# Decode attention with a gated FFN on one core: engine programs as loops over quarter heads, and the FFN moved ahead of the last head's values

## The chip, the cores and the metric

The kernel runs on one core of one Trainium2 chip. The metric is the device time of one execution in microseconds (us). The profile is one execution recorded by the hardware, and its span is about 1.8 us shorter than the device time.

Short names: PE is the matrix engine, DVE the vector engine, ACT the scalar engine, SP the engine that issues the loads. Sixteen DMA engines carry out each load together: in the packet records of the traces each load ends with 16 completions, one from each.

## The reference, cut to what matters

One token attends over a long cache: 16 query heads share 8 key and value heads of 65,536 positions and 256 channels, in bf16. A gated FFN of width 1792 runs on the same normalised token.

```python
# ...
Hq, Hkv, Sk, Dh = 16, 8, 65536, 256
q = (x @ wq)                                      # 16 heads, 2 for each key head
scores = einsum("bhqd,bhkd->bhqk", q, k) * Dh ** -0.5
o = einsum("bhqk,bhkd->bhqd", softmax(scores), v)
a = o.reshape(1, 1, Hq * Dh) @ wo                 # 4096 x 448
# ...
g = silu(x_sel @ w_gate); u = x_sel @ w_up        # 448 x 1792 each
y = (g * u) @ w_down * sigmoid(r)                 # 1792 x 448
return x + a + (xn + y)
```

The caches are 2 x 268 MB and all weights together 12 MB, so 549 MB are loaded once. This is the work; the arithmetic is small.

## The kernel before

Keys and values pass through a ring of four 4 MB slots in SBUF. PE transposes a key slot, ACT and DVE copy the transposes to SBUF, PE multiplies them with the query. A slot is free again when PE has read it, and SP then issues the next load into it. PE's program is a hardware loop over 14 half heads. DVE and ACT run straight-line programs for the whole kernel.

```python
FIRST = [16, 16, 32]          # the first key slot is loaded in three pieces
LAST = [32, 16, 8, 8]         # the last value slot in four
ORDER = [("k", 0), ("v", 0), ("k", 1), ("v", 1), ("k", 2), ("v", 2), ("v", 3), ("k", 3)]
# ... loads in order: wq, keys, gate and up weights, then by ORDER, then the last head's values, then:
item("wd", w_area[:, 0:WDN], [...all of w_down...], "we0", [("FFN1",)])   # waits for the gate and up matmuls
item("wo_end", w_area[:, WDN:WDN + WON], wo_src(Hkv - 1), "we1")
# ...
def epilogue():
    # ...
    for t in range(NT, NT + 2):                   # the last head, two halves
        for c in range(HC):                       # four value slots each
            pe_V(t, c, t == NT, t == NT + 1)
            # ...
            if t == NT and c == 1:
                pe_ffn1()                         # gate and up: 98 small matmuls
    pe_oT(NT + 1)
    pe_ffn2()                                     # w_down: 14 matmuls of 448 columns
    # ... ATTN of the last head, then RESULT
```

## Time and profile before

| | before |
|---|---|
| device time, median of 4 runs | 1292.44 us (1292.22 to 1292.95) |
| span of the profiled run | 1291.1 us |
| PE, DVE, ACT busy | 72%, 43%, 35% |
| loaded | 549 MB at 425 GB/s over the span |

The next lines are from the page of the kernel before: its busy line of PE, then the 40 equal slices of the span (DMA is the mean busy share of the 16 DMA engines in tenths, GB/s what they moved), then the DMA queues (packets, MB, share of 16 engines).

```profile
PE 934.6 (72%) x9673; PEld 669.9 (52%) x9673; DVE 551.6 (43%) x944; ACT 446.5 (35%) x634; POOL 4.5 (0%) x34
...
DMA  9999999999999999999999999999999999999995
GB/s 404 425 433 424 431 432 430 432 429 431 435 428 434 428 434 432 428 435 426 435 433 429 435 427 432 431 432 435 424 436 429 434 431 427 436 429 434 429 431 243
...
q1 hardware_dynamic: 22034, 549.04, 99.1%
q8 instruction: 15, 0.25, 0.1%
q14 instruction: 14, 0.11, 0.0%
```

The kernel is bound by its loads: the DMA share is 9 tenths or more in every slice but the last, at about 431 GB/s (424 to 436 in the slices but the first and the last). No engine's work in the middle can save time unless it delays a load.

The second reading is the end. These are lines of the timeline of the kernel before (start, duration, engine, line, operation, count, and in brackets the idle time before and what ended it).

```profile
1221.96 3.58 PE L541 MATMUL ps_o<-ring,p_sb 128*4 128x512 bf16 x32 [2.33 <-ACT p_sb L485]
...
1229.93 5.39 PE L624 MATMUL ps_m<-xnT_sb,w_area 128*128 128x2 bf16 x98
...
1278.84 0.60 PE L541 MATMUL ps_o<-ring,p_sb 128*4 128x512 bf16 x4 [0.66 <-DMA ring<-in_A_v_cache_dram]
1279.48 0.69 DVE L557 CAST ob_sb<-ps_o 100x512 bf16<-100x512 f32 x1 [43.54 <-PE ps_o L541]
...
1282.60 5.39 PE L656 MATMUL ps_t<-w_area,hT_sb 128*1 128x448 bf16 x14 [2.10 <-DMA w_area<-in_B_w_down_dram]
...
1287.78 1.08 PE L593 MATMUL ps_s<-w_area,oT_sb 128*1 128x448 bf16 x4
...
1288.90 0.61 DVE L663 TENSOR_TENSOR res_bf<-ps_s,rowsf 1x448 bf16<-1x448 f32 x1 [0.20 <-PE ps_s L593]
1289.54 0.33 SPq L331 DMA_DIRECT2D out_dram<-res_bf  x1
```

The last head's first value slot is used at 1222 us, ahead of the gate and up matmuls at 1230. After the last piece of values (1278.8) PE waits 2.1 us for w_down, and 14 matmuls of 385 ns (5.39 us / 14) stand between its landing and the result. The time is thus the arrival of the last byte plus a fixed piece of work.

### The profile page before, as it was taken

How to read it: one execution, taken by the hardware profiler on the slowest of the kernel's cores; microseconds unless marked ns; L12 is line 12 of the kernel's file. 1: busy time of each engine (PE TensorE's matmuls, PEld its weight loads, DVE VectorE, ACT ScalarE, POOL GpSimd, SP SyncE). 2: the span in 40 equal slices, each digit the busy share in tenths (PEclk: the TensorE clock that was granted, in tenths of full speed). 3: DMA queues.
4: the chain of work that ended last, by engine and by line, in shares of the span. 5: the costliest groups of instructions: out<-in, count | busy, mean ns of one | idle time of the engine just before them, and what ended most of it. 6: DMA issues, size and time to landing. Idle time of an engine off the chain costs nothing.

```text
span 1291.1 us, 21412 instructions
## 1 busy us (share of the span) xinstructions
PE 934.6 (72%) x9673; PEld 669.9 (52%) x9673; DVE 551.6 (43%) x944; ACT 446.5 (35%) x634; POOL 4.5 (0%) x34
## 2 busy tenths in 40 slices
PE   4988867696666957668587675876669676696665
PEld 4876645464554735546365453654446454474421
DVE  4666435263443625336254352643436353262300
ACT  2556323253332623225233242432424333242300
POOL 1000000000000000000000000000000000000000
PEclk9899879798887988889788897987979888798665
DMA  9999999999999999999999999999999999999995
GB/s 404 425 433 424 431 432 430 432 429 431 435 428 434 428 434 432 428 435 426 435 433 429 435 427 432 431 432 435 424 436 429 434 431 427 436 429 434 429 431 243
DMA packets 22067, 549.40 MB, mean 426 GB/s; under 512 B 2323, under 2 KB 4374, under 8 KB 4886
## 3 DMA queue, kind: packets, MB, share of 16 engines
q1 hardware_dynamic: 22034, 549.04, 99.1%
q8 instruction: 15, 0.25, 0.1%
q14 instruction: 14, 0.11, 0.0%
q10 hardware_dynamic: 4, 0.00, 0.0%
HBM read 549.03 MB, written 0.00 MB: 425 GB/s over the span
## 4 chain that ended last, share of the span: by engine, by line
DMA 76%; PE 22%; DVE 1%; ACT 0%; issue 0%; SPq 0%; ACTq 0%
DMA ring<-in_A_k_cache_dram 42%; DMA ring<-in_A_v_cache_dram 31%; PE ps_t L382 13%; PE ps_o L541 4%; PE ps_q L416 3%; DMA w_area<-in_B_w_down_dram 3%; DMA wr_row<-in_B_w_r_dram 0%; PE ps_s L449 0%; PE ps_t L656 0%; PE ps_m L624 0%; DVE kt_buf L370 0%; ACT S_sb L494 0%; SPq L328 0%; PE ps_m L593 0%; ACT L494 0%
## 5 line engine op out<-in xcount | busy, mean ns | idle before, releaser
L382 PE MATMUL ps_t<-ident_f,ring 128*128 128x128 f32 x4096 | 578.0, 299 | 218.5 <-DMA ring<-in_A_k_cache_dram 217.1
L370 DVE COPY kt_buf<-ps_t 128x1024 bf16<-128x1024 bf16 x768 | 491.9, 685 | 475.8 <-PE ps_t L382 473.6
L382 PEld LDWEIGHTS ps_t<-ident_f,ring 128*128 128x128 f32 x4096 | 502.9, 154 | 343.6 <-DMA ring<-in_A_k_cache_dram 238.5
L372 ACT ACTIVATE kt_buf<-ps_t 128x1024 bf16<-128x1024 bf16 x256 | 261.8, 1023 | 353.3 <-PE ps_t L382 352.9
L394 ACT ACTIVATE s<-ps_q 98x512 bf16<-98x512 f32 x256 | 152.7, 596 | 319.6 <-PE ps_q L416 319.6
L541 PE MATMUL ps_o<-ring,p_sb 128*4 128x512 bf16 x2048 | 158.4, 462 | 108.6 <-DMA ring<-in_A_v_cache_dram 98.4
L416 PE MATMUL ps_q<-kt_buf,q_cur 128*2 128x512 bf16 x2048 | 169.0, 407 | 0.7 <-ACT s L394 0.7
L541 PEld LDWEIGHTS ps_o<-ring,p_sb 128*4 128x4 bf16 x2048 | 52.2, 95 | 203.1 <-issue 144.9
L557 DVE CAST ob_sb<-ps_o 100x512 bf16<-100x512 f32 x15 | 10.4, 692 | 184.4 <-PE ps_o L541 184.4
L449 PEld LDWEIGHTS ps_s<-sel_bf,s 128*128 128x128 bf16 x1024 | 64.5, 99 | 11.4 <-issue 6.9
L449 PE MATMUL ps_s<-sel_bf,s 128*128 128x8 bf16 x1024 | 64.0, 168 | 0.5 <-ACT s L394 0.5
L485 ACT ACTIVATE p_sb<-S_sb 128x128 bf16<-128x128 bf16 x64 | 17.1, 303 | 101.7 <-PE ps_o L541 101.5
L416 PEld LDWEIGHTS ps_q<-kt_buf,q_cur 128*2 128x2 bf16 x2048 | 26.2, 79 | 6.9 <-ACT s L394 1.2
L514 DVE RECIPROCAL rs<-ps_m 128x4 f32<-128x4 f32 x15 | 2.7, 182 | 45.8 <-PE ps_m L521 45.8
L593 PE MATMUL ps_m<-wo_cur,oT_sb 128*1 128x448 bf16 x56 | 15.4, 406 | 0.0
L494 ACT ACTIVATE S_sb<-S_sb,negmax 128x512 bf16<-128x512 bf16 x16 | 13.3, 860 | 5.1 <-DVE negmax L477 5.1
L521 PEld LDWEIGHTS ps_m<-rowsum,ones_f 128*128 128x128 f32 x60 | 8.6, 207 | 7.4 <-issue 7.4
L429 DVE CAST S_sb<-ps_s 128x512 bf16<-128x512 f32 x16 | 10.9, 681 | 1.9 <-PE ps_s L449 1.9
L431 DVE TENSOR_REDUCE m1p<-S_sb 128x2 f32<-128x512 bf16 x16 | 11.0, 686 | 0.6
L469 PE MATMUL ps_m<-ident_f,m 128*2 128x128 f32 x15 | 4.2, 277 | 9.0 <-DVE m L437 9.0
L585 DVE TENSOR_TENSOR rowsf<-ps_m,rowsf 1x448 f32<-1x448 f32 x14 | 8.6, 612 | 4.6 <-PE ps_m L593 4.3
L521 PE MATMUL ps_m<-rowsum,ones_f 128*128 128x2 f32 x60 | 9.9, 270 | 0.0
(68 smaller groups left out, 91.6 us busy)
## 6 DMA issues: line engine op xcount, KB each, us to landing
ring<-in_A_k_cache_dram SPq DMA_DIRECT2D x63, 4096.0 KB, 33.6
ring<-in_A_v_cache_dram SPq DMA_DIRECT2D x63, 4096.0 KB, 30.4
w_area<-in_A_wq_dram SPq DMA_DIRECT2D x1, 3584.0 KB, 11.4
wo_cur<-in_A_wo_dram SPq DMA_DIRECT2D x7, 448.0 KB, 25.6
ring<-in_A_k_cache_dram SPq DMA_DIRECT2D x2, 1024.0 KB, 14.5
ring<-in_A_k_cache_dram SPq DMA_DIRECT2D x1, 2048.0 KB, 20.9
ring<-in_A_v_cache_dram SPq DMA_DIRECT2D x1, 2048.0 KB, 30.3
w_area<-in_B_w_gate_dram SPq DMA_DIRECT2D x1, 1568.0 KB, 39.0
```

The costliest lines, as they stand in the source:

```text
L370: op(e, ("EV", s, m), lambda x: x.tensor_copy(out=kt[:, :], in_=tb[:, :]), f"ev{m}")
L372: op(e, ("EV", s, m), lambda x: x.activation(out=kt[:, :], in_=tb[:, :], func=ACTF.Copy), f"ev{m}")
L382: ins = nc.tensor.matmul(ps_tf[m][:, jj * P:(jj + 1) * P], lhsT=kv[:, j + GN * m + jj, :], rhs=ident_f[:, :], is_transpose=True, start=Tru ...
L394: op("act", ("EVQ", s), lambda e: e.activation(out=s2[s % 2][0:QROWS, :], in_=ps_q[0:QROWS, :], func=ACTF.Copy), "evq")
L416: ins = nc.tensor.matmul(ps_q[32 * m:32 * m + rep, 0:512], lhsT=q_cur[:, hf, :], rhs=kt[:, :].rearrange("p (k f) -> p f k", f=NH)[:, hf, : ...
L431: op("dve", ("SMAX", b), lambda e: e.tensor_reduce(out=m1p[:, :, k], in_=S.rearrange("p n i -> p i n"), axis=AX.X, op=ALU.max))
L449: ins = nc.tensor.matmul(o, lhsT=s2[s % 2][:, jj * P:(jj + 1) * P], rhs=sel_bf[:, :, :], start=True, stop=True)
L485: op("act", ("PC", t, c), lambda e: e.activation(out=p_sb[:, c, :, :], in_=S_sb[t // 2 % 2][:, n:n + CH, :], func=ACTF.Copy), "pc")
L494: op("act", ("EXPI", h, i), lambda e, i=i: e.activation(out=S[:, :, i], in_=S[:, :, i], func=ACTF.Exp, bias=negmax[:, i:i + 1], scale=1.0, ...
L521: ins = nc.tensor.matmul(ps_m[0:P, C_TOT + f * rep:C_TOT + (f + 1) * rep], lhsT=ones_f[:, :], rhs=rowsum[:, :], start=True, stop=True)
L541: ins = nc.tensor.matmul(ps_o[32 * g:32 * g + 2 * rep, :], lhsT=p_sb[:, c, o + j:o + j + 2, :].rearrange("p n i -> p (n i)"), rhs=kv[:, j: ...
L593: ins = nc.tensor.matmul(dst, lhsT=oT_sb[:, hf, i:i + 1], rhs=wo[:, i, hf, :], start=(hf == 0 and i == 0), stop=(hf == NH - 1 and i == rep ...
```

## The change

The intent: shrink the programs of PE, DVE and ACT to hardware loops over quarter heads (two key and two value slots a turn), do the FFN and half of w_down before the last head's values, and leave only half of w_down and the last output weights for the end. The diff is a rewrite; its core:

```diff
-FIRST = [16, 16, 32]
-ORDER = [("k", 0), ("v", 0), ("k", 1), ("v", 1), ("k", 2), ("v", 2), ("v", 3), ("k", 3)]
+HC = 2                                    # slots in a quarter head
+    LOOPS = {"pe": {"A": 2, "B": 1, "C": 2}, "dve": {"B": U}, "act": {"B": U}}
# ... each engine's program is a list; what is named in LOOPS is emitted as a hardware loop:
#     A: keys of the first head; B: 28 turns; C: values of the last head; U = 4 quarters
+    for t in range(NT):                   # loads of a turn
+        slot_item("k", t + U, 0)
+        slot_item("v", t, 0)
+        slot_item("v", t, 1)
# ...
+        slot_item("k", t + U, 1)
# ... w_down in two halves: wd_a early, wd_b behind the last values
+            item("wd_a", [(wd_a[:, :], wd_src(0), "wd")])
+    item("wd_b", [(w_area[:, 0:WDN], wd_src(1), "we0")], [("FFN1",)])
+    for i in range(rep):
+        item(("wo_end", i), [...])
# ...
+    def middle():                         # before the last head's values
+        pe_m1t(NU - 1)
# ...
+        pe_bc(NU - 1)
+        pe_ffn1()                         # now moving form: 28 matmuls of 448 columns
+        pe_tot(NT)
+        pe_ffn_hT()
+        pe_ffn2(0, "wd_a", wd_a)
# ...
+    def ending():
+        dve_ob(T)
+        pe_oT(T)
+        pe_ffn2(1, "wd_b", w_area)        # 7 matmuls
```

As emitted, the straight programs had 1925 (DVE) and 1194 (ACT) instructions, PE's 2361. The changed ones have 748, 478 and 1362; DVE's loop body has 408, ACT's 253, PE's turn 378. These counts are taken before the build, which shortens the programs: DVE's loop body of 408 is 196 in the compiled program.

## The prediction

> **What bounds the kernel now.** The transfers. The slices give a mean DMA share of 0.9 or more in all slices but the last, at 424 to 436 GB/s; the queue table gives 99.1% of 16 engines' span to the one load queue (549 MB). PE is busy 72%, DVE 43%, ACT 35%. Work inside a half head is off the critical path while ring slots are freed in time; only the two ends count and what delays the slowest of the 16 DMA engines.
>
> **The end before (timeline).** The last V piece lands at 1278.8 us; the output transpose is done at 1280.7. PE then waits for w_down, landing at 1282.55, does 14 matmuls of 448 columns in 5.39 us (375 ns each, PEclk 0.5), four output matmuls; the result leaves at 1289.5. In the windows the DMA rate falls from 416 to 25 GB/s between 1275 and 1281, while one engine works until 1283. Ordering the packet records by completion, the slowest engine is 1.9 us behind the median at 250 us and 5.8 us at 1200; the four steps of about 1 us fall where 8 KB instruction packets are recorded (677/689, 830/859, 1060/1082, 1218). [...]
>
> **Change, costed.**
> 1. Half of w_down is multiplied before the last head's values. After w_down lands, 7 matmuls instead of 14: -2.6 us.
> 2. DVE and ACT loops should stop the fetches between 120 and 1200 us: the slowest engine ends about 3 us earlier. PE's code halves too. Bytes stay equal; w_down's first half moves forward, which puts the last V 1.8 us later.
> 3. The moving-form FFN (28 matmuls of 448 columns, 5.2 us warm, 10.5 us cold, against 98 in 5.4 us), transposes and half of FFN2 (1.3 to 2.6) now stand before the first V slot of the last head. I estimate that slot freed at 1234 to 1240 instead of 1225.5. The engines run dry at about 1235 to 1238: a DMA gap of 0 to 4 us.
> 4. The first K slot is no longer split: PE starts about 6 us later, but transfers are queued to about 57 us. Nothing.
> 5. Each quarter drains the K pipeline (2 to 3 us of PE per 38.9 us of loads) and adds branches; PE's 28% slack takes it.
>
> Sum: -2.6 - 3 + 2 = -3.6 us. Predicted 1289.0 us (1285.5 to 1294.0). Faster by over 2%: 0.01; within 2%: 0.97; slower by over 2%: 0.02.
>
> **What would show it.** DMA share stays full and 431 GB/s between 40 and 1230; fewer instruction packets; the slowest engine's lag stays near 2 us; a dip of DMA share around 1235 to 1243; only 7 w_down matmuls after the last V; result leaving 3 to 5 us earlier.
>
> **What would make it wrong.** [...] A longer DMA gap at the last head (cold PE) loses most of the gain. If PE at 2.5 to 3.6 us a set plus the drains can't keep 38.9 us a quarter, the whole middle slows: the only way to over 2% slower.

The packet times in it (677, 689 and so on) count from the trace's own start, some 11 us before the profile's zero. Its "424 to 436 GB/s" leaves out the first slice too (404).

Two passages are cut from it: one on how programs are fetched, one on the risk of a loop body that is too long, put at 3 to 7 us and not in the sum. No term of the sum is cut: it came to -3.6 us, as printed. The figures that no line of the trace gives are estimates: the -3 us for the fetches (most of the 3.9 us by which the lag grows from 250 to 1200 us), the 1.8 us of delay (0.8 MB at 431 GB/s), the 5.2 us (28 times half of the 375 ns), the 57 us (23.7 MB issued by 17.8 us, at 431 GB/s), the 38.9 us (16.8 MB at 431 GB/s), PE's 2.5 us a set (28 matmuls; 224 in the 20 us from 40 to 60, at a granted clock of 1.00) and, with no numbers named, the 3.6 us a set, the drains of 2 to 3 us and the slot at 1234 to 1240 us. That PE starts about 6 us later was measured afterwards: its first key matmul begins at 22.87 us in the changed kernel and at 16.84 us before.

## The result

| | before | changed |
|---|---|---|
| median | 1292.44 us (1292.22 to 1292.95) | 1285.18 us (1285.14 to 1285.25) |
| ratio | | 0.9944 (95%: 0.9930 to 0.9958) |
| last load byte, us after the first packet | 1281.5 | 1275.8 |
| from there to the end of the device time | 11.0 us | 9.4 us |
| slowest DMA engine behind the median, at about 1220 us | 5.75 us | 1.30 us |
| recorded instruction packets | 15 + 14 | 8 + 6 |

Ratios are the mean time of one kernel's fast runs over that of the other's of the same rounds, so not quite the ratio of the medians. The last three rows are worked out from the packet records of the trace: a 4-byte completion write by each of the 16 DMA engines ends each load, and the lag is the last of the 16 against their median (in the kernel before the completions of one load were up to 7.9 us apart, the fastest 2.2 us ahead of the median and the slowest 5.75 behind). The row "from there to the end" is the median device time less the row above it, which comes from the profiled run; it includes a constant for the start and end of the execution, so only differences between kernels mean something. It also mixes a median with one run; within the two profiled runs alone, the time from the last byte to the end of the span is 7.8 us before and 5.8 us changed, 2.0 us less.

The change gained 7.3 us (0.56%), twice what was predicted, and 0.3 us outside the range. The lines of the changed kernel's page that answer to those above:

```profile
PE 924.9 (72%) x9824; PEld 671.5 (52%) x9824; DVE 585.8 (46%) x1091; ACT 459.2 (36%) x655; POOL 4.5 (0%) x35
...
GB/s 405 427 433 427 433 432 431 430 431 432 432 433 431 433 430 433 430 433 430 433 432 432 432 431 432 429 433 433 431 432 432 432 430 433 431 431 433 431 429 318
...
q1 hardware_dynamic: 22210, 549.04, 99.6%
q8 instruction: 8, 0.13, 0.0%
q14 instruction: 6, 0.05, 0.0%
```

The busy shares have not fallen; DVE's has even risen. The rate in the slices is the same, but the last slice moves 318 GB/s instead of 243: the engines finish more nearly together, and the tail without loads is 2.0 us shorter. Instruction packets fell from 29 to 14. And the timeline of the changed kernel, around the last head and at the end:

```profile
1214.44 6.96 PE L352 MATMUL ps_t<-w_area,xnT_sb 128*2 128x448 bf16 x28
...
1223.74 1.47 PE L352 MATMUL ps_t<-wd_a,hT_sb 128*1 128x448 bf16 x5 [0.36 <-DVE hT_sb L625]
...
1225.45 7.51 PE L352 MATMUL ps_o<-ring,p_sb 128*4 128x512 bf16 x106
...
1275.08 0.60 PE L352 MATMUL ps_o<-ring,p_sb 128*4 128x512 bf16 x4 [0.67 <-DMA ring<-in_A_v_cache_dram]
1275.73 0.69 DVE L540 CAST ob_sb<-ps_o 100x512 bf16<-100x512 f32 x1 [52.14 <-PE ps_o L352]
...
1276.94 2.77 PE L352 MATMUL ps_t<-w_area,hT_sb 128*1 128x448 bf16 x7 [0.20 <-DMA w_area<-in_B_w_down_dram]
1279.51 1.70 PE L352 MATMUL ps_s<-wo_end,oT_sb 128*1 128x448 bf16 x4
...
1281.25 0.61 DVE L727 TENSOR_TENSOR res_bf<-ps_s,rowsf 1x448 bf16<-1x448 f32 x1 [0.82 <-PE ps_s L352]
1281.89 0.32 SPq L776 DMA_DIRECT2D out_dram<-res_bf  x1
```

The FFN's 28 matmuls took 6.96 us, between the prediction's estimates for the full clock ("warm", 5.2 us) and for half of it ("cold", 10.5 us, 28 times the 375 ns at a granted clock of 0.5): the windows grant 0.53 and 0.62 from 1214 to 1218 us and 1.00 from 1218 to 1224. w_down's second half landed at 1276.9, 5.7 us earlier than w_down did before, and seven matmuls instead of 14 followed. The result left 7.65 us earlier (1289.54 less 1281.89).

### The profile page after: what moved, and what is told of

Same layout as the page of the kernel before. It is cut to its first block, busy times and chain, and to the rows that moved or that the text cites. A ratio compares the mean times of both kernels' runs of the same rounds, so it can differ in the third digit from the quotient of the medians.

```text
span 1283.4 us, 22878 instructions
## 1 busy us (share of the span) xinstructions
PE 924.9 (72%) x9824; PEld 671.5 (52%) x9824; DVE 585.8 (46%) x1091; ACT 459.2 (36%) x655; POOL 4.5 (0%) x35
## 4 chain that ended last, share of the span: by engine, by line
DMA 68%; PE 31%; SPq 0%; ACT 0%; issue 0%; DVE 0%
DMA ring<-in_A_k_cache_dram 63%; PE ps_t L352 24%; PE ps_q L352 5%; DMA w_area<-in_B_w_down_dram 3%; DMA ring<-in_A_v_cache_dram 2%; PE ps_s L352 1%; PE ps_m L352 1%; SPq L776 0%; ACT s L430 0%; DVE res_bf L727 0%; PE ps_o L352 0%
## 5 line engine op out<-in xcount | busy, mean ns | idle before, releaser
L352 PE MATMUL ps_t<-ident_f,ring 128*128 128x128 f32 x4096 | 568.8, 296 | 248.6 <-DMA ring<-in_A_k_cache_dram 229.5
L352 PEld LDWEIGHTS ps_t<-ident_f,ring 128*128 128x128 f32 x4096 | 494.9, 152 | 354.2 <-DMA ring<-in_A_k_cache_dram 245.5
L352 PE MATMUL ps_o<-ring,p_sb 128*4 128x512 bf16 x2048 | 132.6, 401 | 67.0 <-DMA ring<-in_A_v_cache_dram 67.0
L540 DVE CAST ob_sb<-ps_o 100x512 bf16<-100x512 f32 x29 | 20.0, 691 | 142.8 <-PE ps_o L352 142.8
L576 DVE TENSOR_TENSOR rowsf<-ps_m,rowsf 1x448 f32<-1x448 f32 x28 | 17.1, 612 | 53.8 <-PE ps_m L352 53.8
L352 PE MATMUL ps_m<-wo_cur,oT_sb 128*1 128x448 bf16 x112 | 25.7, 352 | 0.0
L352 PE MATMUL ps_m<-rowsum,ones_f 128*128 128x2 f32 x116 | 17.6, 256 | 0.0
L352 PEld LDWEIGHTS ps_m<-wo_cur,oT_sb 128*1 128x1 bf16 x112 | 9.3, 83 | 13.5
L454 DVE CAST S_sb<-ps_s 128x256 bf16<-128x256 f32 x32 | 12.9, 404 | 4.3 <-PE ps_s L352 4.3
L456 DVE TENSOR_REDUCE m1p<-S_sb 128x2 f32<-128x256 bf16 x32 | 13.5, 421 | 1.1
## 6 DMA issues: line engine op xcount, KB each, us to landing
w_area<-in_A_wq_dram SPq DMA_DIRECT2D x1, 3584.0 KB, 11.3
```

Source lines behind the costliest of these rows:

```text
L352: return pe.matmul(*a, **k)
L454: O("dve", ("SCOPY", u), lambda it: nc.vector.tensor_copy(out=S, in_=ps_sn))
L456: O("dve", ("SMAX", u), lambda it: nc.vector.tensor_reduce(out=m1p[:, :, k], in_=S.rearrange("p n i -> p i n"), axis=AX.X, op=ALU.max))
L540: O("dve", ("OB", t), lambda it: nc.vector.tensor_copy(out=ob_sb[0:OROWS, :], in_=ps_o[0:OROWS, :]))
L576: O("dve", ("RES", t), lambda it: nc.vector.tensor_tensor(out=base_f, in0=ps_m[0:1, C_BIG:C_BIG + D], in1=base_f, op=ALU.add))
```

## The experiments

The table gathers what each run left. "Behind" is the lag of the slowest DMA engine at about 1220 us. Times are medians; the two packet counts are those of PE's queue (16 KB packets) and of the other engines' queue (8 KB), as the pages print them.

```
kernel            packets   behind   last byte  device time  difference
before            15 + 14    5.75     1281.5      1292.4       11.0
changed            8 +  6    1.30     1275.8      1285.2        9.4
unroll_both        8 + 19    7.66     1283.5      1292.9        9.4
unroll_dve         8 + 14    7.98     1283.7      1292.8        9.1
unroll_act         8 + 11    3.81     1278.3      1287.5        9.2
unroll_pe_ac      13 +  6    2.27     1276.7      1285.8        9.1
unroll_both_mid    9 + 19    8.00     1283.4      1292.5        9.1
wdown_last         8 +  6    1.24     1275.7      1287.0       11.3
ffn_rep2           9 +  6    1.29     1275.7      1285.1        9.4
ffn_rep5           9 +  6    1.42     1284.7      1294.8       10.0
early_wdown        8 +  6    1.25     1275.6      1284.6        9.0
early_warm         9 +  6    1.71     1276.0      1283.5        7.4
before_first64    16 + 14    5.93     1281.3      1292.0       10.7
loop_real3         8 + 51    5.67     1319.9      1328.9        9.1
```

The theory: the end is the last byte of the slowest DMA engine plus the work that follows it, and instruction fetches delay that engine. Fetches are what the recorded instruction packets are taken for: PE's loops unrolled added five to its queue (q8), DVE's loop unrolled eight to the other (q14). The main rivals: the new order of loads, the tail alone, or the first slot in one piece.

### unroll_both: the loops of DVE and ACT taken back

```diff
-    LOOPS = {"pe": {"A": 2, "B": 1, "C": 2}, "dve": {"B": U}, "act": {"B": U}}
+    LOOPS = {"pe": {"A": 2, "B": 1, "C": 2}, "dve": {}, "act": {}}
# ... and one line that keeps the head's index right in a straight program
```

> The changed kernel, but VectorE and ScalarE run their program unrolled again (2511 and 1493 instructions instead of 748 and 478); PE keeps its loops, and loads, FFN and tail are untouched. Theory F (instruction fetches delay the slowest of the 16 DMA engines): the 8 KB instruction packets come back, about 18 to 20 instead of 6 in their queue, the slowest engine's lag behind the median grows from 1.3 us to 4 to 6 us, the time is 1289 to 1291 us. Rival O (the gain is in the order of the loads and in the tail only): 1285.2 us within 0.5 us.

Measured: 1292.92 us, ratio to before 1.0001 (0.9985 to 1.0018). The whole gain is gone, the tail's share with it: the lag is now larger than in the kernel before (7.66 us against 5.75). From the page of this run:

```profile
q8 instruction: 8, 0.13, 0.0%
q14 instruction: 19, 0.16, 0.0%
```

Thirteen packets of 8 KB, 0.11 MB in all, came back and the last byte came 7.7 us later. Mean bandwidth cannot explain it: 0.11 MB at 431 GB/s is 0.25 us. The lag of the slowest engine against the median shows why, here by the load's number and time in the trace:

```
unroll_both   load  48  at  452 us: 0.6     changed   load  48  at  452 us: 0.7
              load  60  at  561 us: 3.3               load  60  at  560 us: 1.3
              load  72  at  669 us: 4.2               load  72  at  668 us: 1.3
              load  84  at  777 us: 5.2               load  84  at  776 us: 1.3
              load  96  at  893 us: 6.2               load  96  at  893 us: 1.3
              load 108  at 1001 us: 7.2               load 108  at 1001 us: 1.3
```

(Load 48 is a small weight load, where the lag shows smaller; two loads later it is 2.3 and 1.3.) The lag grows by 1.0 us from row to row, about every 110 us, and one series of instruction packets has nearly that spacing: 608, 725, 841, 959, 1072 us. Between such steps the lag stays as it is: in the changed kernel 1.3 us from 561 to 1001 us, in the kernel before 3.81 us from 912 to 1040 us. The loads leave no gap meanwhile (DMA share 1.00 from 40 to 1230 us in the changed kernel), and an engine that has lost 1 us did not get it back here. The rival "order of loads and tail alone" falls; the expected size (1289 to 1291) was too small.

### unroll_dve and unroll_act: which engine's program

Each keeps one of the two loops.

> The changed kernel with only VectorE unrolled again; ScalarE and PE keep their loops. In unroll_both the slowest engine's lag grew in steps of 1 us about every 110 us, the spacing of one of the two series of 8 KB instruction packets, the one that fits VectorE's 46 instructions a quarter. Theory F: that series alone comes back (about 8 to 9 packets more than the changed kernel's 6), the lag at 1226 us is 7 to 8 us, and the time is that of unroll_both, 1291.5 to 1293 us. If both series load the same DMA engine: about two thirds of it.

> The changed kernel with only ScalarE unrolled again. Theory F: about 5 more instruction packets, on another DMA engine that was not the slowest: its lag grows to at most 5 us behind its own start, the slowest engine's lag stays at 1.3 to 3 us, time 1285 to 1287.5 us.

Measured: DVE unrolled, 1292.81 us; ACT unrolled, 1287.51 us (the time at the upper end of its expected range, 1287.5, and the lag of 3.81 us 0.8 above its own: ACT's packets delay an engine too). The line of the DMA queue of unroll_dve, then of unroll_act:

```profile
q14 instruction: 14, 0.11, 0.0%
```

```profile
q14 instruction: 11, 0.09, 0.0%
```

DVE's eight packets alone (8,192 bytes each; the straight program is 1015 compiled instructions longer than its loop) cost what both did: 7.6 us, a lag of 7.98 us. ACT's five cost 2.3 us with a lag of 3.81. The two do not add up: the costs fall on different DMA engines, and only the slowest one counts. The 16 completions of one load show it. In unroll_dve at 1213 us one engine is 7.98 us behind the median and the next 0.80; in unroll_both at 1212 us two lag, by 7.66 and 3.66 us, and the third by 0.85. This also answers the rival that straight-line programs are slow for another reason, for instance issue. In unroll_dve the packets of DVE's series recorded at 372.7, 482.9, 599.2, 714.2, 830.4 and 947.9 us of the profile are each followed, within the next load or two, by a step of 0.9 to 1.1 us in this one engine's lag; the one at 1060.5 is followed by 0.6 us and the last, at 1178.0, by nothing. Most DVE packets thus cost their engine about 1.0 us although the packet record itself lasts 0.32 to 0.33 us; no run shows what the rest is.

### unroll_pe_ac: PE's own program

```diff
-    LOOPS = {"pe": {"A": 2, "B": 1, "C": 2}, ...
+    LOOPS = {"pe": {"B": 1}, ...
```

> The changed kernel with PE's loops over the first keys and over the last values unrolled (1965 instead of 1362 instructions), the quarter loop kept. Theory F: 4 to 5 more 16 KB packets in PE's queue, on an engine that is not VectorE's: the mean engine loses 0.3 us, the slowest engine's lag grows by 0 to 2 us, time 1285.2 to 1287 us. If PE's packets land on the slowest engine: 4 to 5 us slower.

Measured: 1285.77 us, lag 2.27 us, five more packets of 16 KB. PE's shorter program was worth about 0.6 us; the slowest engine's lag grew by 1.0 us and not by five, so most of its packets load DMA engines other than the slowest.

### unroll_both_mid: a gap that costs nothing

unroll_both shows a dip of the DMA share at the last head. Lines of the windows of unroll_both: the stretch in us and its length, then busy us and counts of PE, PEld, DVE, ACT and POOL, then PEclk, DMA share and GB/s.

```profile
1232.00:1234.00 2.00, 2.00 (x23) 0.67 (x21) 0.00 (x0) 0.00 (x0) 0.00 (x0) 0.50 0.77 305
1234.00:1236.00 2.00, 2.00 (x37) 0.71 (x33) 0.00 (x0) 0.24 (x1) 0.00 (x0) 0.85 0.22 90
1236.00:1238.00 2.00, 2.00 (x44) 0.86 (x40) 0.00 (x0) 0.38 (x2) 0.00 (x0) 1.00 0.96 293
```

The late engine lands the last keys late, so the FFN ends late, so the first value slot of the last head is freed late, and most engines run dry. Is this gap part of the 7.7 us? The edit puts the FFN behind the first two value slots:

```diff
         pe_bc(NU - 1)
-        pe_ffn1()
         pe_tot(NT)
-        pe_ffn_hT()
-        pe_ffn2(0, "wd_a", wd_a)
 # ... after the first two value slots (PE's loop C unrolled):
+        pe_ffn1(); pe_ffn_hT(); pe_ffn2(0, "wd_a", wd_a)
```

> unroll_both, with the FFN put back behind the first two value slots of the last head (PE's loop over those slots unrolled for it). In unroll_both the DMA progress of the mean engine lost 3.4 us between 530 and 540 MB, at the last head. Theory G (a late engine lands the last keys late, the FFN then frees the value slot too late, and all engines run dry): the 3.4 us are not lost, and the time is that of the lag alone: 1287.5 to 1290.5 us, 2 to 5 us faster than unroll_both. Rival L (the lag alone costs the 7.7 us): 1292.9 us as unroll_both.

The same stretch of unroll_both_mid:

```profile
1234.00:1236.00 2.00, 2.00 (x12) 0.81 (x10) 1.14 (x2) 0.56 (x2) 0.00 (x0) 1.00 1.09 459
```

The gap is gone and the time is not: 1292.46 us, last byte 1283.4 instead of 1283.5. My theory G fell, and rival L stood. At 0.22 of the share some engines still worked in the gap; the engine that sets the end had its backlog and lost nothing. So a hole in the mean DMA share, 0.22 here, cost nothing while the slowest engine had work.

### ffn_rep5 and ffn_rep2: when a late slot does cost

```diff
-                for n, (rr, c) in enumerate(todo):
+                for n, (rr, c) in [z for r_ in range(6 if b0 == 0 else 1) for z in enumerate(todo)]:
# ... and the matmul's start flag
# ffn_rep2: 3 instead of 6; every pass restarts the sum, so the result is right
```

> The changed kernel, with the 14 gate matmuls run six times instead of once (five times in vain, the same result): 13 to 18 us more PE work ahead of the last head's first value slot. In the changed kernel the slot is free at about 1227 and the engines run dry at 1234 to 1236. Theory G: about 7 us of slack, so a gap of 6 to 11 us: 1290 to 1296 us, with a dip of the DMA share about 1236 to 1246. If slots are queued deep enough, or the FFN is off the critical path at any length: 1285.2 us.

> The changed kernel with two extra gate passes instead of five. The five cost 9.5 us and delayed the first value slot by about 13 us (PE at full clock, 2.6 us a pass), so the slack is about 3.5 to 4 us after the landing of queued loads is counted; two passes are 5.2 us. Theory G (a slot freed before the queue runs dry costs nothing, later it costs one for one): 1 to 2 us slower than the changed kernel, 1286 to 1287.5 us. If the cost is proportional from the first pass: 3.8 us slower, 1289 us.

Measured: five extra passes 1294.77 us, 9.6 us more than the changed kernel's 1285.18; two extra passes 1285.10 us, nothing. SP's longest wait, which is for this slot, in the waits of SP from 1200 us on, first the changed kernel and then ffn_rep5 (total, times, longest):

```profile
SPq L776 <- PE ps_o L352: 25.2, 4, 18.6
```

```profile
SPq L776 <- PE ps_o L352: 34.3, 4, 30.2
```

And the windows of ffn_rep5:

```profile
1234.00:1236.00 2.00, 1.78 (x11) 0.89 (x9) 0.99 (x3) 0.00 (x0) 0.00 (x0) 1.00 0.13 53
1236.00:1238.00 2.00, 0.91 (x10) 0.68 (x11) 0.76 (x3) 0.00 (x0) 0.00 (x0) 1.00 0.00 0
1238.00:1240.00 2.00, 2.00 (x36) 0.85 (x38) 0.00 (x0) 0.00 (x0) 0.00 (x0) 1.00 0.00 0
```

SP's wait begins at about 1210 us in both, behind the issue before it, so the slot came free at about 1228.7 in the changed kernel and at 1240.8 with five passes, 12 us later (my expectations say 1227 and 13). There all engines were dry, the share is 0.00, and the last byte came 8.9 us later. With two passes the FFN's 28 matmuls became 56 and took 12.05 us instead of 6.96, but SP issues the load into the slot at 1231.8, only 3.1 us later, as the matmuls behind the FFN then ran at a granted clock of 1.00 and not 0.57; the last byte did not move. So at least 3.1 us of slack lay before this slot, and about 3.3 if the cost beyond it is one for one (12.2 less 8.9, an estimate). A slot freed late thus cost nothing up to 3.1 us (ffn_rep2), and 8.9 us of last byte at 12.2 us (ffn_rep5), as theory G had it. I had expected this run to be 1 to 2 us slower; what was wrong is that two passes would delay the slot by 5.2 us, and the slack of 3.5 to 4 was nearly right.

### wdown_last: the tail by itself

```diff
-            item("wd_a", [(wd_a[:, :], wd_src(0), "wd")])      # with the gate and up weights
+    item("wd_a", [(wd_a[:, :], wd_src(0), "wd")])              # behind the last values
 # ... in middle():
-        pe_ffn2(0, "wd_a", wd_a)
 # ... in ending():
+        W_item("pe", "wd_b")
+        pe_ffn2(0, "wd_a", wd_a)
         pe_ffn2(1, "wd_b", w_area)
```

> The changed kernel, but all of w_down is loaded after the last values, and all 14 of its matmuls run after its landing, as before. Theory T (the tail gain is the 7 matmuls of 375 to 395 ns): 2.5 to 2.8 us slower than the changed kernel, 1287.7 to 1288.0 us, result leaving 2.5 us later. If the tail was worth nothing: 1285.2 us. If it was worth the whole of the 7.3 us: 1292 us.

Measured: 1287.03 us median (1285.95 to 1287.28), 1.85 us slower than the changed kernel. Its timeline at the end:

```profile
1276.88 2.77 PE L352 MATMUL ps_t<-wd_a,hT_sb 128*1 128x448 bf16 x7 [2.07 <-DMA w_area<-in_B_w_down_dram]
1279.45 2.82 PE L352 MATMUL ps_t<-w_area,hT_sb 128*1 128x448 bf16 x7
1282.06 1.22 PE L352 MATMUL ps_s<-wo_end,oT_sb 128*1 128x448 bf16 x4
...
1283.96 0.32 SPq L777 DMA_DIRECT2D out_dram<-res_bf  x1
```

The seven extra matmuls took 2.8 us, but in this run the four output matmuls behind them took 1.22 us instead of 1.70, which fits a clock that rose meanwhile (1.70 us is the changed kernel's at a granted 0.50; in the kernel before they took 1.08 us, at 0.96 from 1288 to 1289 us). So the tail is worth 1.9 us on the median, not 2.6. The difference column says the same: 11.3 against 9.4; the profiled runs alone say 2.1. My expectation of 2.5 to 2.8 was missed. The end varies with the granted clock in any case: in loop_pad2, which compiled to the changed kernel's program (see below), the clock rose at 1279.7 us and the end took 5.1 us from the last byte instead of 5.8.

### before_first64: the start

```diff
-FIRST = [16, 16, 32]
+FIRST = [64]
```

> The kernel before, with its first key slot loaded in one piece as the changed kernel does: PE starts about 6 us later, transfers are queued to about 57 us. The prediction's step 4: no change, ratio to before 1.000 within 0.0005. If the start was on the critical path: up to 6 us slower.

Measured, in the kernel before: 1292.00 us, ratio 0.9997 (0.9984 to 1.0011). No change, as expected. The interval is about 1.7 us wide on each side: it rules out the 6 us, not a change of a us.

### unroll_pad2 and loop_pad2: void

Both put register moves before each operation, to lengthen the programs.

> As unroll_both, with two idle register moves before each VectorE and ScalarE operation of the quarter-head turns: 4415 and 2585 instructions, no data touched. Theory F: about 12 more instruction packets than unroll_both[...], the slowest engine lags by 7 to 11 us, time 2 to 6 us above unroll_both. Rival I (unrolled programs are slow for another reason than fetching, for instance issue):[...] same time as unroll_both.

> The changed kernel with loops, with two register moves before each operation in the VectorE and ScalarE loop bodies: bodies of 680 instead of 408 and 409 instead of 253 instructions. [...] Theory F[...] 12 to 25 more instruction packets than the changed kernel's 6, time 1288 to 1292 us[...]. If [...]moves cost nothing and nothing is fetched: 1285.2 us and 6 packets.

(Theory F's case is a DVE body that is fetched again on each of its 7 turns.)

Measured: 1292.98 and 1285.17 us, with exactly the packets of unroll_both and of the changed kernel (19 and 6). The build removes moves whose register nobody reads: the compiled list of DVE's operations is as long as without them (1413 instructions straight, 196 in the loop body, with and without the moves). So nothing was tested, and neither run counts for or against a theory.

### loop_real3: a loop body three times as long

The same question with real instructions, in DVE's loop only:

```diff
             if kind == "o":
+                if e == "dve" and here_b[0]:
+                    for _ in range(3):
+                        npad[0] += 1
+                        nc.vector.memset(pad_d[0:1, npad[0]:npad[0] + 1], 0.0)
                 fn(it).then_inc(sems[sem], weight[key])
```

> The changed kernel with three 1x1 memsets before each operation in VectorE's loop body (about 165 compiled instructions before, about 570 now), result unaltered. [...] 4 to 5 packets on each of 7 turns, 25 to 35 instruction packets instead of 6, the slowest engine's lag over 10 us, time 1293 to 1310 us. If the loop still fits: 6 packets; time 1285 to 1288 us, the rest from VectorE's longer evictions at the last head.

(The condition of its first case: the longer body is fetched again on every turn. "Still fits" stands for a body that is not.)

Measured: 1328.94 us, ratio to before 1.0287 (1.0270 to 1.0304), 43.8 us above the changed kernel, the result right. The page of loop_real3, then DVE's waits:

```profile
GB/s 406 426 432 430 430 431 432 431 384 396 438 430 428 348 426 437 431 427 379 436 432 428 435 295 437 431 427 436 379 432 426 437 431 344 432 429 435 431 412 279
...
q14 instruction: 51, 0.42, 0.1%
```

```profile
DVE pad_d L781 <- issue: 38.1, 6, 6.9
DVE kt_buf L408 <- issue: 29.3, 6, 4.9
```

The 136 operations of the body got 408 memsets of 59 ns. Their own time is not the cause: DVE's busy time rose only from 585.8 to 623.4 us, DVE is far from the bottleneck, and the slices between the six dips move 426 to 438 GB/s, as without memsets. What is new is twice six waits for nothing that the profile shows, of up to 6.9 and 4.9 us, on six turns, and 51 packets instead of 6. The two stalls of one turn, from DVE's timeline:

```profile
609.90 0.12 DVE L781 MEMSET pad_d<- 1x1 bf16 x3 [5.87 <-issue]
...
615.56 0.69 DVE L408 COPY kt_buf<-ps_t 128x1024 bf16<-128x1024 bf16 x1 [4.89 <-issue]
```

Instruction packets are recorded at 607.9 and 613.7 us, each 2 us before one of these stalls ends, so what DVE waits for is its instructions. While DVE stands still, PE has nothing to do (busy 0.00 us from 612 to 616), no key slot comes free, and then the loads run dry (DMA share 0.35 from 620 to 624): rates of 295 to 396 GB/s in the slices with a dip. With a compiled body of 604 instructions 45 packets more were recorded and DVE stalled on six of its 7 turns; the changed kernel's body is 196 (my expectation said about 570 and 165), and there one packet of 8 KB was recorded between 250 and 1230 us, at 690 us of the trace's time. So the longer body was fetched again turn after turn and the shorter one was not. Where between 196 and 604 this begins was not located.

The repeated packets that I expected are there; my expectation had the sizes wrong: 51 packets, not 25 to 35; a lag of 5.7 us, not over 10; and a cost of 43.8 us where 1293 to 1310 us meant 8 to 25, because of the stalls and not of the lag.

### early_wdown and early_warm: versions that beat both kernels

If the end is the last byte plus what follows, shorten what follows. early_wdown loads and multiplies four more of w_down's blocks early. SBUF use is unchanged, as the last output weights move into the unused end of the weight area.

```diff
+    wd_c = S_("wd_c", [P, 4 * D], BF16)
-    wo_end = S_("wo_end", [P, WON], BF16)
+    wo_end = w_area[:, WGN:WGN + WON]
+            item("wd_c", [(wd_c[:, :], wd_src(1)[:, 0:4 * D], "wd")])
 # ... in middle():
+        pe_ffn2(1, "wd_c", wd_c, 0, 4)
 # ... in ending():
-        pe_ffn2(1, "wd_b", w_area)
+        pe_ffn2(1, "wd_b", w_area, 4, 7)
 # early_warm adds, after the value slots and pieces of the last head (10, 3, 0, 1, 3 times):
+   mm(ps_q[0:2, 0:512], lhsT=ident_bf[:, 0:2], rhs=kt_buf[7][:, 0:512], start=True, stop=True)
```

> The changed kernel unaltered, to compare the three others of this call on the same chip: 1285.2 us within 0.5 us, lag of the slowest engine at 1226 us 1.3 us.

> The changed kernel, with four more of w_down's fourteen row blocks loaded and multiplied before the last head's values (wo_end moves into the unused end of the weight area, so SBUF use is equal). After the last transfer three w_down matmuls are left instead of seven, bytes equal, 0.46 MB moved forward puts the last V piece about 1.1 us later. Theory (time is the last byte plus what follows it; seven matmuls take 2.77 us): 1.0 to 1.5 us faster than the changed kernel, 1283.7 to 1284.2 us. If the output transpose chain after the last V piece (1.9 us) bounds the end instead: under 0.5 us.

> early_wdown, with idle 512-column matmuls after the value slots of the last head, so that PE is busy between the last pieces (PEclk was 0.5 from 1274 to 1282 us in the changed kernel). If the granted clock then stays at 1.0, the last 3 + 4 matmuls take 190 ns instead of 375 to 395 ns each: a further 1.0 to 1.5 us. If the clock stays at 0.5 the idle matmuls only delay the last pieces: same or up to 1 us slower than early_wdown.

Measured: the changed kernel 1285.29 us (1285.13 to 1285.60), early_wdown 1284.58 us (1284.30 to 1284.70), early_warm 1283.46 us (1283.07 to 1284.07). early_wdown gained 0.7 us, between its theory and its rival. Its end:

```profile
1277.52 1.28 PE L356 MATMUL ps_t<-w_area,hT_sb 128*1 128x448 bf16 x3
...
1278.60 1.70 PE L356 MATMUL ps_s<-w_area,oT_sb 128*1 128x448 bf16 x4
```

The last piece of values is used at 1275.93 instead of 1275.08, and the three matmuls begin right behind its transposes, without a wait for w_down: the chain of the last values, not the landing of w_down, now sets when they start. The end of early_warm, which gained another 1.1 us, as expected:

```profile
1277.69 0.73 PE L356 MATMUL ps_t<-w_area,hT_sb 128*1 128x448 bf16 x3
...
1278.25 0.92 PE L356 MATMUL ps_s<-w_area,oT_sb 128*1 128x448 bf16 x4
...
1279.87 0.32 SPq L790 DMA_DIRECT2D out_dram<-res_bf  x1
```

The four output matmuls took 0.92 us instead of 1.70. In the changed kernel PE waits 9.4, 6.1 and 6.4 us between the slots, and the windows grant mostly 0.50 there (0.50 from 1238 to 1250, 0.58 and 0.66 in the next two stretches of 10 us). But after 1.00 from 1270 to 1272 the clock falls once more, to 0.50 from 1274 to 1282, with waits of only 1.3 and 1.4 us before. So long waits alone do not account for the low clock; what sets it was not shown. With the idle matmuls the windows grant 1.00 from 1272 to 1281. early_warm is 0.9932 of the kernel before and 1.8 us (0.14%) faster than the changed kernel.

## Why the prediction was wrong

Its sum was -2.6 for the tail, -3 for the fetches, +2 for a gap. By the table the measured 7.3 us are 5.7 us from an earlier last byte and the rest, 1.6 us, from a shorter tail.

1. **Bound by the loads, only the ends and the slowest DMA engine count: right.** The drains and branches that the change adds to PE in mid kernel changed nothing (427 to 433 GB/s in every slice but the first and the last), and every kernel with the changed tail but ffn_rep5 and early_warm ends 9.0 to 9.4 us after its last byte. (ffn_rep5's 10.0 is a profiled run 0.7 us faster than the median; within that run the end is the changed kernel's 5.8 us.)
2. **The tail, -2.6 us: right in kind, smaller in size.** Alone it is worth 1.85 us (wdown_last; 2.1 by the profiled runs), since the later matmuls partly ran faster: the four output matmuls took 1.22 us in wdown_last and 1.70 in the changed kernel.
3. **The fetches, -3 us: mechanism right, size wrong. This term failed.** The last byte moved by 5.7 us. The lag fell from 5.75 to 1.30 us, so 4.45 us and not 3. I had also named a delay of 1.8 us of the last values by the forward move of half of w_down, though it is not in the sum; a reordering with equal bytes does not move the last byte (wdown_last and early_wdown: 1275.7 and 1275.6). The rest, about 1.2 us, is the progress of the mean engine; the mean engine was 2 us earlier at 500 MB. 15 fewer packets of 1 us over 16 engines are 0.9 us of these 2 by an estimate (unroll_both's thirteen cost it 0.7 us there), and what made the other half is not settled: neither the order of loads as a whole nor the load count was tried alone.
4. **The gap, 0 to 4 us, taken as +2: wrong; the second term that failed.** There was none. The slot was free at about 1228.7 us, not 1234 to 1240: the FFN took 6.96 us and not up to 10.5, as only its first eight or nine matmuls ran at a granted clock of 0.5 (about 375 ns apart) and the rest at 1.0 (about 190 ns), and the last keys no longer waited for a slow engine (in unroll_both, where they did, the load into the slot was issued at 1235.8 and the gap was there). ffn_rep2 shows at least 3.1 us of slack, ffn_rep5 shows that beyond it the cost is real. And unroll_both_mid shows that even a visible gap can cost nothing.
5. **The first slot in one piece, nothing: right** (before_first64).
6. **Drains and branches, nothing: right**, with loop bodies as short as the changed kernel's (DVE's 196 compiled instructions). They were not tried alone; the slices in 1 are what shows it.
7. **The risk of a long loop body: real, but named too small.** I said 3 to 7 us; loop_real3 shows 43.8 us. The prediction's "only way to over 2% slower" was thus wrong too: this is another.

The range ended at 1285.5 and the measured median is 1285.18. It was too narrow on the good side because both wrong terms pointed the same way.

## What to carry to other kernels

In a kernel bound by loads, ask when the slowest DMA engine finishes, not how busy the mean one is: the instruction fetches of PE, DVE and ACT rode on these engines here, and a long straight program cost time here that no busy share shows (DVE's: eight packets, 7.6 us). Put long programs into hardware loops with short bodies, and check the packet count in the profile: here DVE's body of 196 compiled instructions was not fetched again turn after turn (6 packets in its queue), and one of 604 was (51 packets) and stalled its engine by up to 6.9 us at a time. Then shorten what follows the last byte, and see which clock PE is granted there: the last four matmuls took 0.92 us with idle matmuls ahead of them (early_warm) and 1.70 us without.
